# Gate logits of a convolution and mixture-of-experts kernel: transposed tokens as the stationary side, gate columns moving

## The chip, the cores and the metric

One core of one Trainium2 chip. The time is device microseconds of that core from the first to the last instruction of one launch; each time quoted is the median of its runs. The runs of this study fell on several chips, and the kernel before takes 711 us on some of them and 842 us on others. So kernels are compared only with runs of the kernel before made on the same chip in the same call. A ratio is the mean time of one kernel's fast runs over the mean of the other's fast runs of the same rounds, so it is not quite the ratio of the medians. Fast means within 1.5% of the fastest run of the same kernel.

## The reference, cut to what matters

```python
# convolution: x (8, 3584, 192) fp32, a softmax-weighted causal window of 7 per head of 24 features
# then, with x of shape (28672, 192):
logits = x @ w_gate                        # (N, 8)
e_idx  = argmax(logits, axis=1)            # one expert per token
gate_w = softmax(logits)[n, e_idx]
eom    = sigmoid(x @ w_output_gate)        # (N, 8)
out[n] = gate_w * eom[n, e_idx] * (relu(x[n] @ w1[e_idx]) @ w2[e_idx])
```

The part at issue is the two products with 8 columns each, 16 columns in all, for 28,672 tokens of 192 features.

## The kernel before

The tokens go through in 16 units of 1,792. `front_a` makes the convolution (L292), transposes it into `tt` (L306), and makes the logits. `front_b` chooses the experts, and GpSimd scatters the rows to a list per expert in DRAM. The expert matmuls (L553, L555, L572) run on slots of 512 rows loaded from those lists. In the main loop a unit has 16 steps: each does a quarter of one slot, and draws one piece of `front_a` of the unit after next and one of `front_b` of the next.

The logits. A unit's 16 blocks of 112 tokens are taken in pairs; a pair has 384 features, transposed as three chunks of 128. The gate columns, padded from 16 to 32, are the stationary side, and four matmuls run at once in four column tiles of the array (in the trace four records of L315 start within 20 ns of each other at 118.73 us, and the next four 0.40 us later). The result has tokens along the free side, so it is copied out and transposed back:

```python
        for g in range(6):                       # transposes of the tokens
            pt = pft()
            ... # four transposes (L306)
            evac(tt[:, g % 3, (g // 3) * 4 * BT:(g // 3 + 1) * 4 * BT], pt[:, 0:4 * BT])
            yield
        pl = pft()
        for i in range(2):
            for g in range(4):
                nc.tensor.matmul(pl[32 * g:32 * g + 32, 0:4 * BT],          # L315
                                 wg[:, (g // 2) * 2 + i, :],
                                 tt[:, g // 2 + i, (g % 2) * 4 * BT:(g % 2 + 1) * 4 * BT],
                                 start=(i == 0), stop=(i == 1), tile_position=(0, 32 * g))
        lt = pct.tile([128, 4 * BT], FP32, tag="lt", name="lt")
        evac(lt, pl[:, 0:4 * BT])
        yield
        pg = pft()
        for j in range(4):
            nc.tensor.matmul(pg[0:BT, j * 128:(j + 1) * 128],               # L324
                             lt[:, j * BT:(j + 1) * BT], identf,
                             is_transpose=True, start=(j == 0), stop=(j == 3))
        ... # VectorE copies pg to gb
```

`evac` copies PSUM to SBUF, on ScalarE and VectorE by turns (on ScalarE alone during the first three units):

```python
    def evac(o, i):
        sync_flip[0] ^= 1
        if sync_flip[0] or fill[0] is not None:
            nc.scalar.copy(out=o, in_=i)
        else:
            nc.vector.tensor_copy(out=o, in_=i)
```

The main loop, cut:

```python
    for u in range(1, NU):
        todo = []
        for e, bap, inv in plans.pop(u):
            base = reg(bap, [ET.SP], E * CAP - TT)
            todo.append((e, inv, slot_load(base, u)))     # two transposing loads each, on SyncE
        fa, fb = ...                                      # front_a(u + 2), front_b(u + 1)
        for k, (e, inv, xab) in enumerate(todo):
            s = Slot(xab, w_at(e * WE), inv)
            for q in range(4):
                s.first(q)                                # L553, L555
                drain(fa, 1)
                if prev is not None:
                    prev.second(q)                        # L572
                live = drain(fb, 1)
                emit_in(len(pend))                        # scatters of rows, GpSimd
                emit_out(5 if live and pos > 3 else 0)    # pos = 4 * k + q; scatters of results, GpSimd
            prev = s
```

## Time and profile before

| on the chip of the prediction | before |
|---|---|
| time, median of 3 runs | 842.51 us (834.65 to 852.21) |
| PE busy | 686.1 us, 81% of the span |
| VectorE, ScalarE, GpSimd busy | 48%, 43%, 49% |
| granted TensorE clock, mean | 0.919 |
| time at half clock | 138 us |
| one unit in the main loop | 47.7 us |

PE's busy time says which engine is fullest, but the ends of matmuls are modelled by the profile, and the records overlap (those of L553 and L555 at 118.00 to 118.42 us last 0.38 us and start 0.21 us apart), so what a group of instructions costs is read from the timeline: from the start of the matmul before it to the start of the one after. The row PEclk of the page gives the granted clock of each slice in tenths; in the records behind it the clock is either full or half, and a halved period of this trace lasts 3.41 us or a multiple of that (3.41 us at 172.6 us, 6.83 at 220.4, 17.07 at 70.2); only the last one, which runs to the end of the records, is not. The prediction shows the lines.

### The profile page before, as it was taken

How to read it: one execution, taken by the hardware profiler on the slowest of the kernel's cores; microseconds unless marked ns; L12 is line 12 of the kernel's file. 1: busy time of each engine (PE TensorE's matmuls, PEld its weight loads, DVE VectorE, ACT ScalarE, POOL GpSimd, SP SyncE). 2: the span in 40 equal slices, each digit the busy share in tenths (PEclk: the TensorE clock that was granted, in tenths of full speed). 3: DMA queues.
4: the chain of work that ended last, by engine and by line, in shares of the span. 5: the costliest groups of instructions: out<-in, count | busy, mean ns of one | idle time of the engine just before them, and what ended most of it. 6: DMA issues, size and time to landing. Idle time of an engine off the chain costs nothing. (4 is left out here: it accounts for less than half of the span.)

```text
span 844.8 us, 14071 instructions
## 1 busy us (share of the span) xinstructions
PE 686.1 (81%) x4948; PEld 445.5 (53%) x4948; DVE 406.4 (48%) x1307; ACT 365.8 (43%) x581; POOL 410.8 (49%) x425
## 2 busy tenths in 40 slices
PE   3881988989697988989797988979598995949844
PEld 1540565647364655747464665647365664626632
DVE  7561744547281735538272746538272654512130
ACT  0672443445252543535353543435253552525521
POOL 2145174545446463545545464545546455545541
PEclk9996998999898997999898998989799998969987
DMA  8978694534434152434435152434313123143110
GB/s 178 249 162 138 99 190 101 139 84 123 98 103 125 41 158 57 126 99 118 108 88 133 41 144 73 134 82 121 101 39 101 54 68 87 58 118 77 39 37 9
DMA packets 132359, 86.59 MB, mean 102 GB/s; under 512 B 88427, under 2 KB 122455, under 8 KB 132288
## 3 DMA queue, kind: packets, MB, share of 16 engines
q1 hardware_dynamic: 102656, 42.35, 21.6%
q0 software_dynamic: 28736, 43.31, 19.9%
q8 instruction: 39, 0.64, 0.3%
q14 instruction: 32, 0.26, 0.1%
q10 hardware_dynamic: 896, 0.03, 0.1%
HBM read 35.80 MB, written 44.43 MB: 95 GB/s over the span
## 5 line engine op out<-in xcount | busy, mean ns | idle before, releaser
L479 POOL DMA_INDIRECT out_dram<-y,oi x260 | 257.3, 990 | 232.7 <-issue 125.0
L561 ACT ACTIVATE ht<-pp 128x1024 f16<-128x1024 f32 x195 | 199.5, 1024 | 156.2 <-PE pp L555 108.0
L553 PE MATMUL pp<-xa,wres 128*128 128x512 f16 x520 | 206.2, 397 | 37.2 <-DMA xa<-xcg_sorted 21.8
L572 PE MATMUL pyt<-wres,ht 128*128 128x192 f16 (+1 forms) x2080 | 225.6, 253 | 5.2 <-DVE ht L559 4.4
L572 PEld LDWEIGHTS <-ht 128*128 128x128 f16 x2080 | 185.7, 100 | 73.4 <-issue 40.7
L459 POOL DMA_INDIRECT xcg_sorted<-xs,du x128 | 134.5, 1051 | 180.0 <-ACT xs L280 90.7
L555 PE MATMUL pp<-xb,wres 128*128 128x512 f16 x520 | 204.6, 394 | 5.0 <-DMA xb<-xcg_sorted 5.0
L583 ACT COPY y<-pyt 128x384 f32<-128x384 f32 x130 | 62.5, 480 | 202.6 <-PE pyt L572 118.4
L292 PE MATMUL pf<-xt,band 118*112 118x384 f32 x256 | 109.3, 519 | 16.0 <-DMA xt<-in_x_dram 12.7
L559 DVE TENSOR_SCALAR ht<-pp 128x1024 f16<-128x1024 f32 x65 | 79.3, 1220 | 68.9 <-PE pp L555 45.7
L553 PEld LDWEIGHTS <-wres 128*128 128x128 f16 (+1 forms) x520 | 52.2, 100 | 63.8 <-issue 31.3
L555 PEld LDWEIGHTS <-wres 128*128 128x128 f16 (+1 forms) x520 | 52.6, 101 | 52.7 <-issue 23.8
L315 PE MATMUL pf<-tt,wg 128*32 128x448 f32 x256 | 54.2, 566 | 26.6 <-issue 22.3
L586 DVE TENSOR_SCALAR oi<-pyt 128x4 uint32<-128x4 f32 x65 | 10.6, 162 | 128.8 <-ACT y L583 107.6
L441 PE MATMUL pf<-xrow,pm 112*128 112x194 f16 x512 | 65.1, 247 | 6.6 <-DVE pm L425 4.5
L292 PEld LDWEIGHTS pf<-xt,band 118*112 118x112 f32 x256 | 46.6, 189 | 44.2 <-DVE band L133 13.8
L420 DVE TENSOR_TENSOR xrow<-cv,gs 112x384 f16<-112x384 f32 x128 | 64.9, 547 | 0.0
L282 DVE COPY tt<-pf 128x448 f32<-128x448 f32 x41 | 25.5, 623 | 81.4 <-PE pf L315 45.8
L425 DVE TENSOR_SCALAR pm<-pos,pos 112x256 f16<-112x256 f16 x256 | 61.3, 301 | 0.0
L306 PEld LDWEIGHTS pf<-identf,cv 112*128 112x128 f32 x384 | 43.7, 141 | 18.3 <-DVE cv L282 2.5
L306 PE MATMUL pf<-identf,cv 112*128 112x112 f32 x384 | 51.5, 260 | 0.9 <-ACT cv L280 0.5
L280 ACT COPY cv<-pf 112x384 f32<-112x384 f32 x74 | 34.0, 479 | 40.1 <-PE pf L292 16.7
(132 smaller groups left out, 447.0 us busy)
## 6 DMA issues: line engine op xcount, KB each, us to landing
xt<-in_x_dram SPq DMA_DIRECT2D x8, 1344.0 KB
xt<-in_x_dram SPq DMA_DIRECT2D x8, 1260.0 KB
out_dram<-y,oi POOLq DMA_INDIRECT x260
wres<-in_moe_w_dram POOLq DMA_DIRECT2D x8, 384.0 KB
wres<-in_moe_w_dram POOLq DMA_DIRECT2D x8, 256.0 KB
xcg_sorted<-zrow SPq DMA_DIRECT2D x8, 256.0 KB
xcg_sorted<-xs,du POOLq DMA_INDIRECT x128
xa<-xcg_sorted SPq DMA_TRANSPOSE x65
```

The lines of the kernel that those rows point to most:

```text
L292: nc.tensor.matmul(pc[0:BT, 0:NB * GH], band[0:KI, h, :], xt[0:KI, :, h * GH:(h + 1) * GH], start=True, stop=True)
L306: nc.tensor.matmul(pt[:, j * BT:(j + 1) * BT], cvf[0:BT, m * 2 * D + i * 128:m * 2 * D + (i + 1) * 128], identf[0:BT, 0:BT], is_transpose= ...
L420: nc.vector.tensor_tensor(out=xr[P, k:k + 2, 0:D], in0=cv[P, k:k + 2, :], in1=gs[P, k:k + 2].unsqueeze(2).to_broadcast([BT, 2, D]), op=ALU ...
L441: nc.tensor.matmul(ps[:, r * XW:(r + 1) * XW], pm[P, l, r * 128:(r + 1) * 128], xr[P, l * NG + i, :], start=(r == 0 and l == 0), stop=(r = ...
L459: i = nc.gpsimd.indirect_dma_start(out=xcg2, out_offset=bass.IndirectOffsetOnAxis(ap=du[:, i:i + 1], axis=0), in_=xs.rearrange("p r w -> p ...
L479: i = nc.gpsimd.indirect_dma_start(out=out, out_offset=bass.IndirectOffsetOnAxis(ap=oi[:, j:j + 1], axis=0), in_=y[:, j, :], in_offset=Non ...
L553: nc.tensor.matmul(pp[:, j, :], self.w(fc * 128, 128), self.xa, start=True, stop=False)
L555: nc.tensor.matmul(pp[:, j, :], self.w(F + fc * 128, 128), self.xb, start=False, stop=True)
L559: nc.vector.tensor_relu(out=ht, in_=pp)
L561: nc.scalar.activation(out=ht, in_=pp, func=AF.Relu)
L572: nc.tensor.matmul(self.pp[:, o:o + D], self.ht[fc // 2][:, fc % 2, q * 128:(q + 1) * 128], self.w(2 * F + fc * D, D), start=(fc == 0 and ...
L583: nc.scalar.copy(out=self.y[:, q - 1:q + 1, :], in_=self.pp[:, 0:2 * D].rearrange("p (g d) -> p g d", d=D))
```

## The change

The sides are swapped: each chunk of transposed tokens (112 columns) is loaded as weights, and the 16 or 32 gate columns move. The result has tokens along partitions at once. This does away with the column tiles, the copy `lt` and the transposes back.

```diff
-    wg = const.tile([128, 4, 32], FP32)
+    wg = const.tile([128, 4, 16], FP32)
 ...
         pl = pft()
-        for i in range(2):
-            for g in range(4):
-                nc.tensor.matmul(pl[32 * g:32 * g + 32, 0:4 * BT], ... tile_position=(0, 32 * g))
-        lt = pct.tile([128, 4 * BT], FP32, tag="lt", name="lt")
-        evac(lt, pl[:, 0:4 * BT])
-        yield
-        pg = pft()
-        for j in range(4):
-            nc.tensor.matmul(pg[0:BT, j * 128:(j + 1) * 128], ... is_transpose=True, ...)
+        wb = wg[:, 2:4, :].rearrange("p a e -> p (a e)")
+        for m in range(NG):
+            t = slice(m * BT, (m + 1) * BT)
+            o = m * 32
+            nc.tensor.matmul(pl[0:BT, o:o + 16], tt[:, 0, t], wg[:, 0, :],
+                             start=(m == 0), stop=False)
+            nc.tensor.matmul(pl[0:BT, o + 16:o + 32], tt[:, 2, t], wg[:, 1, :],
+                             start=False, stop=False)
+            nc.tensor.matmul(pl[0:BT, o:o + 32], tt[:, 1, t], wb,
+                             start=False, stop=(m == NG - 1))
 ... # the copy to gb is contiguous now; the rows of wg are loaded in another order
```

More of the change, by code (lines that the diff above doesn't have):

```diff
@@ L136 @@
                 data=cw[:, h:h + H // 2, k:k + 1].to_broadcast([128, H // 2, BT]))
-    wg = const.tile([128, 4, 32], FP32)
+    wg = const.tile([128, 4, 16], FP32)
     nc.vector.memset(wg, 0.0)
-    for i, (p0, p1, d0) in enumerate([(0, 128, 0), (0, 64, 128), (64, 128, 0), (0, 128, 64)]):
+    for i, (p0, p1, d0) in enumerate([(0, 128, 0), (0, 128, 64), (0, 64, 128), (64, 128, 0)]):
         nc.scalar.dma_start(wg[p0:p1, i, 0:E], moe_w_gate[d0:d0 + p1 - p0, :])
@@ L312, in front_a @@
         pl = pft()
-        for i in range(2):
-            for g in range(4):
-                nc.tensor.matmul(pl[32 * g:32 * g + 32, 0:4 * BT],
-                                 wg[:, (g // 2) * 2 + i, :],
-                                 tt[:, g // 2 + i, (g % 2) * 4 * BT:(g % 2 + 1) * 4 * BT],
-                                 start=(i == 0), stop=(i == 1), tile_position=(0, 32 * g))
-        lt = pct.tile([128, 4 * BT], FP32, tag="lt", name="lt")
-        evac(lt, pl[:, 0:4 * BT])
-        yield
-        pg = pft()
-        for j in range(4):
-            nc.tensor.matmul(pg[0:BT, j * 128:(j + 1) * 128],
-                             lt[:, j * BT:(j + 1) * BT], identf,
-                             is_transpose=True, start=(j == 0), stop=(j == 3))
+        wb = wg[:, 2:4, :].rearrange("p a e -> p (a e)")
[8 more added lines that the diff above has]
+                             start=False, stop=(m == NG - 1))
         gb = pr.tile([128, NB, 16], FP32, tag="gb", name="gb")
-        nc.vector.tensor_copy(
-            out=gb[0:BT].rearrange("p (l i) e -> p i l e", l=2),
-            in_=pg[0:BT].rearrange("p (i l e) -> p i l e", l=2, e=32)[:, :, :, 0:16])
+        nc.vector.tensor_copy(out=gb[0:BT],
+                              in_=pl[0:BT, 0:NB * 16].rearrange("p (c e) -> p c e", e=16))
         units[u] = cv, gb
```

## The prediction

> **What bounds the kernel now.** I read the page's busy table first, then its forty slices, then the groups with shapes kept apart, then the timeline of PE around the logits.
>
> ```profile
> PE 686.1 (81%) x4948; PEld 445.5 (53%) x4948; DVE 406.4 (48%) x1307; ACT 365.8 (43%) x581; POOL 410.8 (49%) x425
> ...
> PE   3881988989697988989797988979598995949844
> ...
> PEclk9996998999898997999898998989799998969987
> ```
>
> TensorE is the fullest engine by a wide margin, and from slice 5 to slice 38 it is mostly at 7 to 9 tenths. The other engines are half idle. The kernel works in 16 units of 1,792 tokens; each unit runs its front (convolution, transposes, logits, routing) woven into 16 steps of the expert matmuls. From 118 us to 739 us the bursts of expert loads that open a unit are 45 to 50 us apart, mean 47.7 us. The two groups that the change touches, and the two that tell what its new instructions cost, in the groups view of PE and of its weight loads:
>
> ```profile
> L292 PE MATMUL pf<-xt,band 118*112 118x384 f32 x256 | 109.3, 519 | 16.0 <-DMA xt<-in_x_dram 12.7 <-ACT cv L280 3.2
> ...
> L315 PE MATMUL pf<-tt,wg 128*32 128x448 f32 x256 | 54.2, 566 | 26.6 <-issue 22.3 <-DVE tt L282 3.5 <-ACT tt L280 0.7
> ...
> L324 PE MATMUL pf<-identf,lt 128*112 128x128 f32 x64 | 13.4, 347 | 45.1 <-issue 28.7 <-DVE lt L282 14.6 <-ACT lt L280 1.9
> ...
> L292 PEld LDWEIGHTS pf<-xt,band 118*112 118x112 f32 x256 | 46.6, 189 | 44.2 <-DVE band L133 13.8 <-ACT cv L280 6.9 <-issue 5.9
> ...
> L315 PEld LDWEIGHTS pf<-tt,wg 128*32 128x32 f32 x256 | 10.5, 109 | 59.0 <-issue 49.3 <-DVE tt L282 6.1 <-ACT tt L280 3.2
> ```
>
> Two things are to be seen. The logits stand 128 times in the program and 256 times in the trace: each fp32 matmul runs as two records, each with its own weight load. The transposes back (L324) run as one. And 71.7 us of PE's idle time stand just before these two groups, which looks like a prize for whoever removes them. The timeline of PE shows whether it is:
>
> ```profile
> 118.42 0.38 PE L555 MATMUL pp<-xb,wres 128*128 128x512 f16 x1
> 118.73 1.71 PE L315 MATMUL pf<-tt,wg 128*32 128x448 f32 x16
> 120.38 0.83 PE L572 MATMUL pyt<-wres,ht 128*128 128x192 f16 x8
> ...
> 215.34 0.38 PE L555 MATMUL pp<-xb,wres 128*128 128x512 f16 x1
> 223.68 1.10 PE L324 MATMUL pf<-identf,lt 128*112 128x128 f32 x4 [7.96 <-issue]
> ...
> 738.67 0.82 PE L572 MATMUL pyt<-wres,ht 128*128 128x192 f16 x8
> 751.54 0.58 PE L553 MATMUL pp<-xa,wres 128*128 128x512 f16 x1 [12.05 <-ACT ht L561]
> ```
>
> In the unit at 118 us nothing stalls: the logits hold PE for 1.95 us from the matmul before to the matmul after. From then on every unit loses 6 to 9 us at this place, in two alternating ways: PE waits at L324 for the copy `lt` (VectorE makes it), or the sixteen records of L315 crawl over 8 to 10 us (ScalarE makes `lt`). But the unit that starts at 738.77 us has no front at all, no L315 and no L324, and it loses 12 us in the same place. In the timeline of SyncE each of these stalls covers the burst of eight transposing loads (211.62 to 224.00 us, 259.91 to 271.49 us), during which GpSimd issues scatters back to back. In the unit at 259 us the copy of `ht` waits until 264.50 us for a matmul that had ended by the trace at 258.94, two microseconds before the first L315. So the stall belongs to the burst, and L315 and L324 are only where PE happens to be standing.
>
> [...] 32 fp32 columns take 109 ns and 112 take 177 ns (medians of L315 and L292), 0.85 ns a column [...]. [...] 128 fp16 columns load in 96 ns (L579)[...]. [...] The trace shows what tiling gave: 16 records of 539 ns pass in 1.65 us, start to start, as four run at a time. [...] right after the stall of 215 to 223 us a row of eight L572 takes 1.49 us, before it 0.83.
>
> **The change, part by part.** For each unit it removes 8 logit matmuls (16 records), the copy `lt`, and 4 transposes back. It adds 24 logit matmuls, 8 groups of three, each with 112 columns of `tt` as weights and 16, 16 or 32 columns moving.
>
> Removed on PE where nothing stalls: for L315 1.95 us less the 0.21 us of the matmul before it, 1.74; for L324 0.65 less 0.21, 0.44. Together 2.2 us a unit.
>
> Added on PE: 24 fp32 matmuls are 48 records, each with a load of 112 fp32 columns. Moving 32 columns twice at the rate of L292 (384 columns in 0.32 us, so 0.83 ns a column) is 27 ns, and 16 columns are 13 ns: far less than the load. Loads run beside the matmul before (the transposes L306 go every 95 ns with a load between each), so the load sets the pace, 95 ns (an estimate from the slope above, since no place in this trace is bound by fp32 loads). 48 times 95 is 4.6 us. Net +2.4 us of PE a unit, +38 us over 16.
>
> Removed elsewhere: 16 copies of 448 columns, 9 on ScalarE (some 0.53 us) and 7 on VectorE (0.62 us), 9 us in all on two engines that are half idle: worth nothing by itself. The round trip PE, copy, PE is hidden by a step of expert work where nothing stalls, and costs PE some 0.7 us of idle in each of the three start-up units.
>
> Moved: a unit had 23 evacuations, an odd number, so the alternation between ScalarE and VectorE swapped from unit to unit; now it has 22, and the order of instructions shows the same assignment in every unit: all eight `xs` and the last `tt` on VectorE. That is the arrangement of the units where L315 crawled. In them PE stands at the second half of the tiles until VectorE's copy of the last `tt` comes, at the end of the burst. So of the 48 new records 24 can run inside the stall, for nothing, and 24 run after it, on a halved clock: 24 times 190 ns, 4.5 us. Before, 2 slow records of L315 and L324 came after it (1.6 and some 0.6 us): +2.2 us in those six units. In the six others L315, eight L572 and four expert matmuls had run inside the stall and only L324 (0.9 us) after it; now 4.5 us and those expert matmuls (1.5 to 3 us) come after: +5 to 6. Mean +3.9 for 12 units is 47 us; the unit at 118 us gives +2.4, the three start-up units +1 each. That sum is +52 us. Counted at full clock without the stalls it is +38. I take +43: **886 us**.
>
> **Rivals.** First, the stall is caused by the column tiles and goes with them. For: L315 crawls with no semaphore to wait for (gaps of 1.1 and 1.6 us ended by "issue"), and 71.7 us of idle stand before the two lines. Against: the late signals that precede L315, and the last unit. It would give 12 times 7, some 84 us, less 38: about 795 us. I give it 7%.
>
> Second, the new matmuls fit wholly into the stall: PE has 6 to 9 us idle there in 12 units and 4.6 us are to be placed. For: the idle is there. Against: half of them need the last `tt`, which arrives when the stall ends. Only if that copy came early would it be about even, 835 to 855 us.
>
> Third, small matmuls don't count as activity[...]: 3.4 us at half speed lose 1.7 us more in 12 units, 20 us, so some 905 us; and if records crawl in the burst as L315 did, all 48 come after it, 915 us. For: the array streams for 13 to 27 ns of each 95. Against: every halved period of this trace ended within 10 us.
>
> Fourth, ScalarE or VectorE becomes the bound through the fixed assignment: VectorE gains four `xs` of 0.55 us in half of the units; at 48% busy it carries that.
>
> **Range and chances.** The full-clock count gives 880 us, the stalled count 894, the clock rival 905 to 915, the load pace being off by 15% moves 11 us; hiding brings it down to 850. Range 850 to 918. Slower by over 2% (above 859.4 us) 80%, within 2% 13%, faster 7%.
>
> **What would show it.** Right if PE's records grow from 4948 by about 16 times (48 less 20), 448; if the loads of `tt` last about 177 ns and start 95 ns apart at full clock; if a unit grows from 47.7 us to some 50.5; if the stall at each burst is still there, with PE standing inside the new group for the last `tt`. Step one (load-bound pace) is wrong if the spacing is 40 ns or 180 ns. The stall step is wrong, and the prediction with it, if PE runs through the bursts without a gap of 5 us or more.

## The result, and the profile after

The changed kernel is slower: 922.92 us (918.28 to 927.58, 4 runs) against 847.36 us for before on the same chip (4 runs). The ratio is 1.1006, with a 95% interval of 1.0862 to 1.115. Two of the four runs of before (852.21 and 856.37 us) are over 1.5% above the fastest and left out of the ratio, so the loss is 76 us between the medians and 84 us by the ratio. The direction was predicted; the time lies 5 us above the predicted range.

The page of the changed kernel, to be set against the first fence of the prediction:

```profile
PE 759.7 (83%) x5396; PEld 559.8 (61%) x5396; DVE 402.1 (44%) x1300; ACT 359.3 (39%) x572; POOL 406.6 (44%) x425
...
PEclk9885989889697988969698896969889696979986
```

PE's records grew by 448, as counted beforehand. The new thing is the clock: in the main loop the row dips in nearly every unit to 6 or 7, or to 8 in two slices on end, where mostly it dipped to 8 in one before. In the records behind this row the clock is halved for 274 us in all, against 138 us (some 2 us of each lie past the last instruction). The halved periods of the main loop last 14 to 17 us; before they lasted 3 to 10.

The timeline of PE around the group in the unit at 225 us (the third column is the engine; a number in brackets is idle time before the row):

```profile
225.67 0.38 PE L550 MATMUL pp<-xb,wres 128*128 128x512 f16 x1
225.89 0.28 PE L318 MATMUL pf<-wg,tt 128*112 128x16 f32 x2
...
231.32 0.19 PE L318 MATMUL pf<-wg,tt 128*112 128x16 f32 x1 [1.93 <-issue]
...
234.89 0.57 PE L322 MATMUL pf<-wg,tt 128*112 128x32 f32 x2 [1.06 <-issue]
235.28 0.54 PE L318 MATMUL pf<-wg,tt 128*112 128x16 f32 x2
...
240.51 0.56 PE L322 MATMUL pf<-wg,tt 128*112 128x32 f32 x2
240.88 1.47 PE L567 MATMUL pyt<-wres,ht 128*128 128x192 f16 x8
```

The group holds PE from 225.89 to 240.88 us. In the first 9 us 16 of its 48 records go through, with gaps (12 to 18 in the 12 units); then 32 go every 187 ns, and the eight L567 after it still run at half speed (1.47 us against 0.83). All 12 such groups look alike, 14.7 to 15.9 us from the matmul before to the matmul after. The starts of the loads that open the units, from 124.7 to 812.2 us, are now 52.9 us apart in the mean, where they were 47.7: 5.2 us a unit.

### The profile page after: what moved, and what is told of

Its sections match the earlier page's. It is cut to its first block, busy times and chain, and to the rows that moved or that the text cites. A ratio compares the mean times of both kernels' runs of the same rounds, so it can differ in the third digit from the quotient of the medians.

```text
span 918.0 us, 14962 instructions
## 1 busy us (share of the span) xinstructions
PE 759.7 (83%) x5396; PEld 559.8 (61%) x5396; DVE 402.1 (44%) x1300; ACT 359.3 (39%) x572; POOL 406.6 (44%) x425
## 5 line engine op out<-in xcount | busy, mean ns | idle before, releaser
L548 PE MATMUL pp<-xa,wres 128*128 128x512 f16 x520 | 210.2, 404 | 34.8 <-DMA xa<-xcg_sorted 20.1
L567 PE MATMUL pyt<-wres,ht 128*128 128x192 f16 (+1 forms) x2080 | 232.4, 258 | 6.2 <-DVE ht L554 5.5
L567 PEld LDWEIGHTS <-ht 128*128 128x128 f16 x2080 | 193.4, 104 | 65.9 <-issue 31.3
L454 POOL DMA_INDIRECT xcg_sorted<-xs,du x128 | 131.5, 1027 | 189.5 <-DVE xs L283 139.9
L320 PE MATMUL pf<-wg,tt 128*112 128x16 f32 x256 | 59.1, 300 | 27.4 <-issue 27.4
L322 PE MATMUL pf<-wg,tt 128*112 128x32 f32 x256 | 63.5, 327 | 20.9 <-issue 20.9
L318 PE MATMUL pf<-wg,tt 128*112 128x16 f32 x256 | 57.0, 292 | 27.9 <-issue 27.8
L318 PEld LDWEIGHTS pf<-wg,tt 128*112 128x112 f32 x256 | 53.1, 249 | 32.4 <-issue 30.4
L283 DVE COPY tt<-pf 128x448 f32<-128x448 f32 x13 | 8.1, 625 | 146.5 <-remote 145.7
L320 PEld LDWEIGHTS pf<-wg,tt 128*112 128x112 f32 x256 | 53.0, 251 | 28.2 <-issue 28.2
L283 DVE CAST xs<-pf 128x388 f16<-128x388 f32 x108 | 59.8, 553 | 14.6 <-PE pf L436 6.7
L281 ACT COPY cv<-pf 112x384 f32<-112x384 f32 x102 | 47.5, 477 | 46.4 <-PE pf L293 30.4
```

The costliest lines, as they stand in the source:

```text
L318: nc.tensor.matmul(pl[0:BT, o:o + 16], tt[:, 0, t], wg[:, 0, :], start=(m == 0), stop=False)
L320: nc.tensor.matmul(pl[0:BT, o + 16:o + 32], tt[:, 2, t], wg[:, 1, :], start=False, stop=False)
L454: i = nc.gpsimd.indirect_dma_start(out=xcg2, out_offset=bass.IndirectOffsetOnAxis(ap=du[:, i:i + 1], axis=0), in_=xs.rearrange("p r w -> p ...
L548: nc.tensor.matmul(pp[:, j, :], self.w(fc * 128, 128), self.xa, start=True, stop=False)
L567: nc.tensor.matmul(self.pp[:, o:o + D], self.ht[fc // 2][:, fc % 2, q * 128:(q + 1) * 128], self.w(2 * F + fc * D, D), start=(fc == 0 and ...
```

## The experiments

The open question was which part of this loss (77 us in an expectation below, from one run of each kernel) belongs to what: the pace of the weight loads, the halved clock, the waits inside the group, or the fixed assignment of the copies. On three chips (numbered 3, 9 and 12) before took 710 to 713 us, on two (2 and 5) 842 us. The expectations call the latter chips with "late signals": the trace shows an engine waiting for a matmul that had ended 5 to 9 us earlier, as at 264.50 us in the prediction. The text calls them chips with waits. All results were correct.

### e1: the moving side padded, so that the array is busy while weights load

```diff
-    wg = const.tile([128, 4, 16], FP32)
+    wg = const.tile([128, 3, BT], FP32)          # zeros beyond the 16 or 32 gate columns
 ...
+        nc.tensor.matmul(pl[0:BT, 0:352], zrow[:, 0:BT], zrow[:, 0:352], start=True, stop=False)
 ...
-            nc.tensor.matmul(pl[0:BT, o:o + 16], tt[:, 0, t], wg[:, 0, :], ...
+            nc.tensor.matmul(pl[0:BT, o:o + BT], tt[:, 0, t], wg[:, 0, :], ...   # and the other two alike
```

The zero matmul opens the bank over all its columns once, as the padded outputs overlap; what spills over into a neighbour's columns is added there, and is zero; the result of e1 was correct.

> The changed kernel with the moving side of every logit matmul padded with zero columns from 16 or 32 to 112 (and one small fp16 zero matmul to open the bank), so that the array streams for as long as the weights load. Theory 'short matmuls do not count as activity': the records still go every 95 to 100 ns at full clock, but the halved-clock time, 274 us in the changed kernel's profile against 138 before, falls to some 150 to 200 us and the time from 923 to 885 to 905 us. Rival 'only the idle of the stall halves the clock': halved time stays near 270 us and the time within 1% of 923.

Measured: 747.65 us against 711.25, ratio 1.0497 [1.0437, 1.0556]. The halved-clock time of the profile is 47 us. The changed kernel itself on such a chip is e5 below: 1.1111, with 143 us. The times of the expectation were meant for a chip where before takes 842 us; the ratios can be compared. The page of e1, and the timeline of its group:

```profile
PE 679.7 (91%) x5412; PEld 495.4 (66%) x5412; DVE 401.8 (54%) x1300; ACT 360.0 (48%) x572; POOL 406.2 (54%) x425
...
PEclk9998599999999999999999999999999999999987
```

```profile
211.53 0.31 PE L316 MATMUL pf<-zrow 128*112 128x352 f16 x1
211.68 0.36 PE L320 MATMUL pf<-wg,tt 128*112 128x112 f32 x2
...
216.20 0.36 PE L324 MATMUL pf<-wg,tt 128*112 128x112 f32 x2
216.40 0.82 PE L569 MATMUL pyt<-wres,ht 128*128 128x192 f16 x8
```

The 48 records take 4.7 us, 98 ns each as in e5 below, although each moves up to seven times the columns: so it isn't the moving columns that set the pace. What fills the time is the weight loads (PEld is busy for 4.36 of the 4.40 us from 211.50 us, in the windows under e5), and by the author's reading they set it. Yet the clock row is at 9 throughout the main loop, and the expert matmuls after the group run at full speed (eight L569 in 0.82 us). More streaming work made the kernel faster by some 5%: e7 and e8 below are the padded and the unpadded kernel on one chip, 748.12 against 785.57 us.

### e5: the changed kernel beside before on a chip with no waits

No edit.

> The changed kernel, not altered, beside the kernel before on the same chip. On a chip where before takes 711 us and no burst stalls, the paired-load run gave 1.108 of before although its edit moved nothing, so 1.10 to 1.11 is expected: 780 to 790 us, halved-clock time over 100 us. If before takes 842 us here (a chip with the stalls): 920 us. Rival 'the 77 us came from the stalls': 1.03 or less where there are none.

Measured: 789.84 us against 710.48, ratio 1.1111 [1.1051, 1.1171]. On this chip nothing waits at the group, and the change costs 79 us, about as much as on the first chip (76 to 84). So the waits that the prediction spent most of its lines on have little part in the loss. The timeline of the group, without the waits, shows the clock fall inside it:

```profile
213.48 0.28 PE L318 MATMUL pf<-wg,tt 128*112 128x16 f32 x2
213.61 0.35 PE L320 MATMUL pf<-wg,tt 128*112 128x16 f32 x2
...
216.36 0.35 PE L318 MATMUL pf<-wg,tt 128*112 128x16 f32 x2
216.56 0.53 PE L320 MATMUL pf<-wg,tt 128*112 128x16 f32 x2
...
219.54 1.47 PE L567 MATMUL pyt<-wres,ht 128*128 128x192 f16 x8
```

Two records take 0.2 us until 216.56, that is for the first 3.1 us of the group, and 0.37 us from there on. In the windows view (PE busy in us, then the other engines; PEclk is the granted clock) of that unit and of the same stretch of e1:

```profile
213.50:217.90 4.40, 4.40 (x41) 4.40 (x39) 0.16 (x1) 1.02 (x1) 3.19 (x4) 0.85 0.43 109
217.90:222.30 4.40, 4.40 (x22) 3.44 (x23) 0.42 (x1) 0.00 (x0) 3.48 (x4) 0.50 0.64 172
222.30:226.70 4.40, 4.40 (x28) 2.98 (x27) 2.65 (x6) 2.08 (x4) 2.29 (x3) 0.87 0.55 139
```

```profile
211.50:215.90 4.40, 4.40 (x45) 4.36 (x44) 0.19 (x2) 1.02 (x1) 3.25 (x4) 1.00 0.43 108
215.90:220.30 4.40, 4.40 (x36) 3.16 (x35) 2.50 (x6) 1.07 (x2) 3.42 (x4) 1.00 0.70 172
```

PE has no idle time in either. A unit of e5 takes 44.4 us, one of e1 41.3, one of before on such a chip 38.4 (e3, a repeat of before by what its edit did, in the mean of ten units). So of the 6.0 us that a unit grows by, 2.9 come with e1 (the pace) and 3.1 are the clock.

### e9: padded to 64 columns

The same edit as e1 with 64 in place of 112.

> e1 with the moving side padded to 64 columns in place of 112, so that the array streams for some 53 ns of each 98. If activity is judged by a threshold below a half, the clock is kept: ratio 1.05 as e1. If it takes an array that is nearly always streaming: 1.08 to 1.11.

Measured: 749.69 us against 712.85, ratio 1.0525 [1.0479, 1.0571], halved for 41 us:

```profile
PEclk9999599899999999999999999999999999999987
```

By the rate of 0.83 ns a column, read from L292 in the prediction (384 columns in 0.32 us), the array streams an estimated 53 ns of each 98 here, and the clock was kept in the main loop. In the changed kernel it streams an estimated 13 or 27 ns of 98, and the clock fell (143 us halved in e5). Where between these it turns was not measured.

### e6: the group in two halves

The first 12 matmuls go before the fifth set of transposes, two steps earlier, with their own small PSUM tile and copy; the other 12 stay.

```diff
+        def half(m0):
+            pl = pft()
+            for m in range(m0, m0 + 4):
+                ... # the three matmuls of pair m, then a copy to gb[0:BT, 2 * m0:2 * m0 + 8]
         for g in range(6):
+            if g == 4:
+                half(0)
 ...
-        pl = pft()
-        ...
+        half(4)
```

> The changed kernel with its 24 logit matmuls in two groups of 12, the first two steps earlier, with expert matmuls between, so that no stretch of short matmuls is longer than 2.4 us; one more small VectorE copy. [...] the clock is no longer halved by the group, halved time near that of e1 (47 us), ratio 1.04 to 1.06 of before. Rival 'short matmuls halve the clock wherever they stand, or the cost is not the clock': ratio 1.09 to 1.12.

Measured: 754.95 us against 710.48, ratio 1.0603 [1.0542, 1.0664]; the profile has 78 us at half clock, more than the 47 us that were expected:

```profile
PEclk9687579999999999999999999999999999999987
```

All 26 halves of the main loop run at 98 ns a record, and a unit takes 41.1 us, about as in e1. The halved time is in the start-up, where the two halves of a unit stand close together and some run at 187 ns. Nothing about the matmuls was changed, only how many stand in a row: the rows of 2.3 us kept the clock in the main loop (PEclk is at 9 from the seventh slice on, but for the last two), the row of 48 records, 4.7 us at that pace, lost it in e5 (PEclk 0.50 from 217.90 to 222.30 us).

### e10: the group issued twice

On top of e1: the loop over `m` runs twice, with the zero matmul before each, the second overwriting the first.

```diff
-        for m in range(NG):
+        for m in list(range(NG)) + list(range(NG)):
```

> e1 with the whole logit group issued twice (the second overwrites the first, same result), to measure the cost of the group by itself at kept clock. Theory 'PE is the bound and the group costs its own length, 4.7 us, in each unit': ratio of before rises from 1.05 by 0.09 to 0.11, to 1.14 to 1.16. Rival 'part of the group is hidden in idle time of PE': below 1.11.

Measured: 823.67 us, ratio 1.1568 [1.1525, 1.1611]. Against e9, at kept clock, that is 74.0 us more, or 4.6 us for each of 16 groups. In the main loop, from 183 us on, a unit takes 46.2 us, where it takes 41.3 in e9 and e1: 4.9 us more, the whole length of the second group with its zero matmul. So PE is the bound there and nothing of the group hides. Over the whole kernel it is a little less a group, as some of it is won back in the first units.

### e4, e7, e8: the assignment of the copies

e4 is the kernel before with the assignment fixed as in the changed kernel; e7 is e1, and e8 the changed kernel, with the swap from unit to unit restored. Each has one line more in `front_a`:

```diff
+        sync_flip[0] ^= 1
```

> The kernel before with one extra flip of the alternation in each unit, so that each unit assigns its evacuations to ScalarE and VectorE in the same way, as the changed kernel does. Theory 'the new matmuls cost the time': 1.00 to 1.02 of before, 842 to 860 us, with all units of the kind where the logits crawl. Rival 'the fixed assignment costs the time': 880 us or more.

Measured: 718.32 us against 711.25, ratio 1.0098 [1.0056, 1.0139].

> e1 (padded moving side) with the alternation of ScalarE and VectorE swapping from unit to unit again, as in the kernel before. The fixed assignment cost 1.0 per cent in e4, so theory 'the remaining 5 per cent of e1 are load pace plus assignment': ratio 1.035 to 1.045. Rival 'the load pace alone': 1.05 as e1.

Measured: 748.12 us against 710.48, ratio 1.0513 [1.0458, 1.0568], where e1 had 1.0497. The expected gain of 1% isn't there.

> The changed kernel with the swap from unit to unit restored and nothing else. If the assignment adds 1 per cent: 1.09 to 1.10 of before against 1.10 to 1.11 for the changed kernel. If the assignment is what halves the clock: below 1.06.

Measured: 785.57 us against 710.48, ratio 1.1012 [1.0936, 1.1088], where e5 had 1.1111; the intervals overlap. So the fixed assignment costs 1% in the kernel before, and nothing that could be told apart in the changed one, and it is not what halves the clock (145 us in e8, 51 in e7).

### e2, e3: an edit that moved nothing

The loads of a slot were issued one slot ahead of use in place of eight at the head of the unit, in the changed kernel (e2) and in the kernel before (e3).

```diff
-            todo.append((e, inv, slot_load(base, u)))
+            todo.append((e, inv, bap))
 ...
         for k, (e, inv, _) in enumerate(todo):
+            next_load()          # loads slot k + 1
```

> The changed kernel with the eight transposing loads of a unit issued in pairs, one slot ahead of use, in place of eight in a row. Theory 'the burst of eight loads makes the stall': the gaps of 0.7 to 2.2 us inside the logit group go, the group takes 5 to 9 us where it took 15, and the time falls to 840 to 870 us. Rival 'the stall belongs to the logit group itself': the group still takes 14 to 16 us and the time stays at 910 to 930.

> The kernel before with the same pairing of the loads. Theory 'burst': the waits of 6 to 9 us at the transposes back and the crawl of the column-tiled logits go, and the time falls from 842 to 760 to 800 us. Rival 'column-tiled matmuls stall by themselves': within 2% of before.

Measured: e2 785.6 us, ratio 1.1084 [1.1015, 1.1152]; e3 712.96 us, ratio 1.0018 [0.9977, 1.006], both against 711.25. In e2 the profiled run took 772.02 us, and the three of the ratio 784.82 to 793.30, so these count as slow beside it; a ratio of fast runs would rest on one run alone. Neither tests its theory. The trace still has eight loads in a row in every unit (in e3 from 239.65 to 251 us): SyncE issued them ahead of the program's interleaving; and this chip had no waits to remove. They serve as repeats. In e2 the profile has units of both kinds: from 170 to 334 us a unit takes 41.1 us and the group 4.87 us with no record slower than 100 ns; from 377 us on, a unit takes 44.4 us and the group 5.8 to 5.9. So in one run the same instructions lose the clock in some units and keep it in others.

The records of the clock show where the two kinds differ. In each run all halved periods begin on one grid of 3.41 us (3.413 us in the records of the kernel before and of the changed one). Two groups of e2, at 292.83 and at 333.92 us, with the steps of the grid that their second parts fall in and the steps after (PEclk is the third number from the end):

```profile
294.94:298.35 3.41, 3.41 (x37) 3.30 (x37) 0.42 (x1) 0.00 (x0) 2.69 (x3) 1.00 0.60 155
298.35:301.77 3.42, 3.42 (x26) 2.29 (x25) 2.43 (x6) 1.46 (x3) 2.62 (x3) 1.00 0.69 168
335.90:339.31 3.41, 3.41 (x38) 3.41 (x38) 0.42 (x1) 0.00 (x0) 2.80 (x3) 1.00 0.84 180
339.31:342.72 3.41, 3.41 (x16) 2.00 (x14) 1.59 (x3) 0.34 (x1) 2.50 (x4) 0.50 0.71 171
```

The first group ends at 297.48 us and has 2.53 us in its step, and the clock stays. The second ends at 338.57 and has 2.67 us in its step, and the clock is halved for the whole of the next. It was so in all units of the main loops of e2, e5, e6 and e8: where 2.67 us or more of these matmuls fell into one step, the clock was halved at its end; where 2.53 us or less did, it stayed. That is what these four runs had; what lies behind it was not shown. The halves of e6 are 2.29 us long, below both figures; the padded groups of e1, 4.7 us long, fill whole steps and kept the clock. A unit of 41.1 us is 12 steps and 0.14 us, so in e2 the group moved along the grid, 2.13, 2.27, 2.40, 2.53, 2.67 us, until it lost the clock. A unit of e5 takes 44.38 us, 13 steps to within 0.02, so the group fell on nearly the same place each time and lost the clock in every unit.

### e11, e12, e15, e16: transposed tokens and gate columns in fp16

```diff
-        tt = pct.tile([128, 3, NB // 2 * BT], FP32, tag="tt", name="tt")
+        tt = pct.tile([128, 3, NB // 2 * BT], FP16, tag="tt", name="tt")
 ... # and wg copied to fp16 once
```

> The changed kernel with the transposed tokens and the gate columns rounded to fp16: each of the 24 matmuls is then one record with one load of 112 fp16 columns. The result may fail the comparison, as some tokens may choose another expert; that is accepted. Theory 'load pace': records go every 47 to 60 ns, the group takes 1.2 to 1.5 us in place of 4.7, the clock stays up, and the time is 0.97 to 0.99 of before. Rival 'the cost is the number of matmuls': above 1.02.

Measured (changed kernel in fp16, no waits on this chip): 703.73 us against 712.85, ratio 0.9827 [0.9764, 0.9889]. The groups view of weight loads, of e1 and then of e11:

```profile
L320 PEld LDWEIGHTS pf<-wg,tt 128*112 128x112 f32 x256 | 36.2, 178 | 1.1
```

```profile
L320 PEld LDWEIGHTS <-tt 128*112 128x112 f16 x128 | 17.5, 137 | 1.5
```

One record per matmul in place of two, going every 52 ns in place of 98: the group takes 1.2 us, and the clock stayed up in the main loop (PEclk of its page is at 9 from slice 9 to 38). This kernel is 1.7% faster than before; the interval leaves out 1, but with a limit of 2% the verdict is unclear, and on a chip with waits the gain is not there (e15 below). A rounded logit could still send a token to another expert where two logits nearly tie.

> The kernel before with the transposed tokens and the gate columns rounded to fp16, so that the swap can be judged at equal precision against e11 (0.983 of before). Theory 'load pace of fp32': a column-tiled group of 8 fp16 records takes some 0.6 us in place of 1.74, saving about 1.1 us a unit: 0.97 to 0.985 of before, as good as e11 or slightly better, so in fp16 the swap neither costs nor gives over 1 per cent. Rival 'the swap itself gives the gain of e11': 0.99 or more.

Measured (kernel before in fp16, on chip 2, with waits): 841.31 us against 841.88, ratio 0.9969 [0.9919, 1.0019]. This is the number of the rival, but e11 fell on a chip without waits, so the two can't be compared; hence e15 and e16.

> e11 again, beside e16 on one chip. Without late signals 0.983 of before as in e11; with them within 1 per cent of before, as e12 was.

> e12 again, beside e15. Without late signals 0.97 to 0.985, within 1 per cent of e15: in fp16 the swap neither costs nor gives. With them 0.99 to 1.00.

Measured on chip 5, with waits: e15 840.08 us, ratio 1.0000 [0.9932, 1.0069]; e16 824.53 us, ratio 0.9797 [0.9736, 0.9857]. At equal precision on this chip the swap loses 1.9%, against the expected 1% at most, so it isn't the swap that gave e11 its gain. On a chip without waits e16 was not run. The two chips with waits differ in the gain of the same kernel (0.997 and 0.980), and why is not known.

### e14: e1 on a chip with waits

> e1 again. On a chip without late signals 1.05 of before. On one with them: if the clock halved by short matmuls is half of the loss there too, 1.04 to 1.07 against 1.10 for the changed kernel; if the idle of the stall keeps the clock down anyway, 1.08 to 1.11.

Measured on chip 5: 882.86 us against 841.52, ratio 1.0482 [1.0418, 1.0546]. The changed kernel had 1.1006 on a chip of that kind. So also there the padding takes away about half of the loss, as far as two chips can be compared, though PE stands idle inside the group (62.9 us in all before its records, by the page of e14): the groups of e14 still take 13 to 15 us, and what is won is won after them. The profile has 177 us at half clock, against 274 in the changed kernel.

### e13, e17, e18: what makes the waits

In the kernel before on the first chip, and in e12, e13 and e16 on chips 2 and 5, PE waits, mostly for 5 to 10 us, in nearly every unit. e13 gives three buffers to the transposed tokens in place of six, so that the loads cannot come eight in a row.

```diff
-    pxt = ctx.enter_context(tc.tile_pool(name="pxt", bufs=6))
+    pxt = ctx.enter_context(tc.tile_pool(name="pxt", bufs=3))
```

> The kernel before with 3 buffers for the transposed tokens in place of 6, so that a slot's loads must wait until the slot three before has been read and can't come eight in a row. On a chip with late signals, theory 'the burst of eight makes them late': the waits of 5 to 10 us go and the time falls from 842 to 720 to 780 us; rival 'each load does it': the same loss in more and shorter pieces, 830 us or more. On a chip without: within 3 per cent of 711 us, a little slower for loads that come later.

Measured on chip 5, with waits: 842.67 us against 841.52, ratio 0.9995 [0.993, 1.006]. The edit worked and the waits stayed. The timelines of SyncE and of PE in one unit of e13:

```profile
313.42 0.63 SPq L530 DMA_TRANSPOSE xa<-xcg_sorted  x1
315.07 0.60 SPq L532 DMA_TRANSPOSE xb<-xcg_sorted  x1
322.45 1.13 SPq L530 DMA_TRANSPOSE xa<-xcg_sorted  x1
```

```profile
313.38 0.38 PE L555 MATMUL pp<-xb,wres 128*128 128x512 f16 x1
323.02 1.10 PE L324 MATMUL pf<-identf,lt 128*112 128x128 f32 x4 [9.26 <-DVE lt L282]
```

From 316 to 322 us no load is issued at all, and PE waits. So a burst of eight loads isn't needed for the wait, though four loads still stand at its start. In e12 the same waits stand partly before L574 and `ht`, where its shorter group leaves PE (30.2 us of idle time before L574 end with `ht` by its page, 4.4 us before the same matmul, L572, in the kernel before), so they don't belong to the logits either. What remained was the run of scatters by GpSimd, which covers most of the wait in the units looked at (in e13 one every 1.29 us from 308.80 to 320.07 us, of the wait from 313.76 to 323.02). It can't be the whole cause: in e3, on a chip without waits, loads (239.65 to 251 us) and scatters (238.56 to 253.7 us) stand side by side in the same way, and PE is busy throughout. e17 breaks that run up by always holding five scatters back; e18 does both.

```diff
-                emit_out(5 if live and pos > 3 else 0)
+                emit_out(5)
```

> The kernel before, with five output scatters always held back in place of letting all go at the end and the start of a unit, so that GpSimd's runs of scatters are shorter at the place of the waits. On a chip with late signals: if the run of scatters makes them late, the waits shorten and the time falls from 842 to 750 to 820 us; if not, 830 to 850. On a chip without: within 1 per cent of before, and nothing is learnt of it.

> e17 with the loads spread as in e13. On a chip with late signals: if loads and scatters together make them late, 720 to 800 us and clearly below e17; if neither does, 830 to 850 us. On a chip without: within 1 per cent of before.

Measured: 729.94 and 730.93 us against 711.01, ratios 1.0288 and 1.0305. They fell on chip 9, which has no waits, so they say nothing of the cause; holding scatters back costs 3% there, where at most 1% was expected. What makes TensorE's signals late on some chips stays open.

## Why the prediction was wrong

- **The count and the pace of the new records: right.** 48 records a unit were counted and 448 more in all were found. Their pace was estimated at 95 ns and measured at 98, and the moving columns don't set it, as e1 showed by moving up to seven times as many in the same time. At kept clock the change costs 36 us (e1) to 41 us (e14); the prediction said 38. e10 showed that in the main loop every microsecond of the group is on the path.
- **The clock: the step that failed.** The sum took +43 us from two counts, in both of which the clock recovered after the group as it had before. That short matmuls might not count as activity was put among the rivals, sized at 20 us ("3.4 us at half speed lose 1.7 us more in 12 units"), and set aside because "every halved period of this trace ended within 10 us". That reading was wrong: the trace has one of 17.1 us in the start-up (at 70.2 us) and one of 13.7 us in the last unit (at 742.6 us). And the trace held no such group, so its halved periods could not speak for it. What the runs showed in its place: the group itself halved the clock, also where PE never waits (e5: PE busy for all of the 4.40 us from 217.90 us, at a granted clock of 0.50). The term measures 37 us on a chip without waits (e8 less e7), 44 us (1.1111 less 1.0497, times 710), and some 44 us on chips with waits (1.1006 less 1.0482, times 842, from two chips; uncertain by 13). It is as large as the pace, and without it the time would have been near the prediction of 886 us: e14 took 883. That the two are so close is in part luck, as the two counts behind 886 were 38 and 52 us.
- **The range.** A unit grew from 47.7 to 52.9 us, where 50.5 was given as a sign. 918 us stood for the third rival in full. The rival was real and about twice its estimate.
- **24 records for nothing inside the wait: wrong in size.** In the 12 units 12 to 18 went through; in the one at 225 us 16 did, and 32 were left for the half clock, 6.0 us in place of 4.5.
- **The waits.** The warning that they would not go away with L315 and L324 was right, on the first chip and in e12. The cause given, the burst of eight loads, was not borne out: in e13, with four in a row, the waits and the time stayed, and the cause is open. And their role was overrated: on chips where they don't occur the change costs 79 us, about the same.
- **The assignment of the copies.** That all units would have the same one was right, and is seen in the 12 groups alike. Its price can't be told from zero in the changed kernel.

## What to carry to other kernels

Here one record of a logit matmul took 98 ns with 16 to 112 moving columns (e5, e1), beside a weight load of 112 columns, and an fp32 matmul was two such records, each with its load (256 loads for 128 matmuls in e1); in fp16 it was one record, every 52 ns (e11). So count the loads before swapping sides. Then look at how long short matmuls stand in a row: rows of 48 records, 4.7 us at that pace, lost the clock in e5 though the busy row shows PE full, and the half clock fell on the expert matmuls that came next too (eight L567 in 1.47 us against 0.83). Padding the moving side (e1, e9) or splitting the row (e6) kept the clock in the main loop of this kernel, and left only the pace to be paid (ratios of 1.05 to 1.06 against 1.11).
